# One kernel, a new static order: 1,331 operations rearranged, 54 copies moved between two engines, three warm-up matmuls fewer

## The chip, the core and the metric

The kernel runs on one core of a Trainium2 chip. A core has five instruction streams that run side by side and meet at semaphores: TensorE (PE, matmuls; PEld is its weight load), ScalarE (ACT), VectorE (DVE), GpSimd (POOL), and SyncE (SP), which here issues nearly all DMAs. The metric is device time in microseconds (us) of one execution.

## The reference, cut to what matters

Two attention layers on the same input `x` (2048 tokens by 640, bf16, 32 heads of 20), mixed by a gate:

```
g = sigmoid((x * gate_w).sum(-1))
out = g * A(x) + (1 - g) * B(x)

A: q, k, v from x @ wqkv; phi(t) = [softmax(t @ w_phi), softmax(-t @ w_phi)]
   o = phi(q) @ (phi(k)^T v) / (phi(q) @ sum phi(k)), then o @ wo
B: 4 segments of 512 tokens; in each, causal softmax attention inside the segment,
   plus a memory M, z from the segments before: num / den with phi = elu + 1
   o = sigmoid(beta) * a_mem + (1 - sigmoid(beta)) * a_dot, then o @ wo
```

## The kernel before

The kernel writes its program as a graph. `build_all` creates every operation (a matmul group, one copy, one activation, one DMA) with the tiles that it reads and writes, and `schedule` and `emit` turn the graph into five instruction streams. Nothing is decided by a planner at build time: three constants at the top of the file hold the result of a search made beforehand.

- `ORDER` is one list of all operations, numbered in the order in which `build_all` makes them and written in base 36. Each engine runs its own operations in this order, strictly one after the other.
- `CHOICE` has a digit for each operation that two engines could do: 0 is the first engine named, 1 the second. Copies out of PSUM made by `evac` may be on ACT or DVE. The multiplications `ETr` (line 902 scales oP, line 941 adds the memory part moT, line 1104 scales ET) and `Anorm` (line 973) may be on DVE or POOL.
- `WHERE` has a digit for each tile: the buffer that it takes, or the pair of the eight PSUM banks. An operation that writes a tile waits for all readers of the tile that held its place before.

In `emit`, a wait is put in front of an operation for each producer on another engine that is not yet known to have finished, so whatever stands behind that operation on its engine waits too. This holds for the DMA queue on SP as well.

The work, by the names in the code: B needs `qkproj` (five matmuls of 512 columns, line 647, for segment n, head group c, q or k side), `vproj` (ten matmuls, lines 669 and 670), then for each of 8 head groups per segment the bursts `QK` (lines 774), two `exp` per burst on ACT (line 783), `mask` on POOL (line 787), `PV` on PE (line 815) and a copy `oU_ev`. There are 80 bursts and 160 `exp`. A burst takes four PSUM banks until its two `exp` have read them. A needs `pkA`, `vA`, `Aexp`, `Zred` (line 971), `Zrec` (line 972), `Anorm`, `kv`, and the sum of E in `acc`, called `chain` (line 1013). When all keys are done, for each segment S of queries come `pqA` (line 1067), `qexp` (line 1072), the sums `Zq` (line 1084), and a way through DRAM that spreads the quotient of two sums over the partitions: `Zq_ev`, DMA `zw`, DMA `zr`, `rq` (lines 1095 and 1096, DVE), four DMAs `rw`, one DMA `rr`, `ETr`, and then the matmuls `U` (line 1119) with `Uc` and `Uo` on DVE. `Nmm` (lines 925 and 926), `memc` and `memp` (lines 930 to 933) read the memory of B. `final` (lines 1145 and 1146) is the output projection of one of 16 tiles of 128 tokens; the four of the last segment are split into `finA` and `finB`, joined on DVE (`oadd`, line 1160). `spin` (line 1168) is a matmul of 512 columns whose result nobody reads.

The set-up loads `B_wq` and `B_wk` through `stq` and `stk`, each in a first part (head groups 0 and 1) and a second part (groups 2 to 4), spreads them into `WB` by copies `WBm` and `WBs`, and loads `B_wv` into `WvB`.

Of the kernel before, what the change touches and what calls it, by code (L numbers as in the profile page):

```python
# [36 lines left out]
2w 2x oz oh 78 4s 4t 4u 2p 4x ow 4v oi oj 4z 3j 4j 4y 8a p2 p0 3i 3o 3m 3n 3p 56 79 8b 92 4k qj qk 57 p8 58 77 p1 p9 pb pc 19 51 om on 59 53 52 54 7w
88 5g os 7x 50 ot 5i 76 89 ok 5h 5j 55 7a 5c 5k 7b 5e dq 5d 5f ol 5a dr 67 69 p3 68 7c q8 di q9 dj oo qa pj p4 5l 80 pk 5m 5b 7e pd 5o 5n pe pf 81 5q
5p qd 8c pg 8d 5x pl pv 5y 5z 10r 60 ph pi 5r 5s pw 5t 86 25 5u 87 qe 84 63 64 85 65 pm 7f 6a 6b 7g pn po qg qh pp pq pr ps pt qi ds 8g pu px dt 66 8e
5v py 5w qb 6c qc 6d l pz 6y 61 62 70 6z q0 71 ql q1 6j q2 26 6l 8m do 8n 7d c8 7h 6k 8o 6m qm dp qn 7i 6o 6q 8f 7j dk 1b ca 6p 6f c9 6h 4w q5 dw q6  # L40
qf 1f 6n dl 6r q3 q4 6g 6u dx cb 6i 6w q7 dy 6s 6v 6x qu 8h 1d dz 9c 9e r6 1e 72 6t r7 9d 95 qr 98 qt qv qo 96 qq qs qp 9a 99 cc cd qw 73 e0 74 9r 9t
9s 8p ce qx 8q e1 97 re 8r rf 9h 8i 8s j6 9i 9f 94 qy cg 9j 9k 6e 8t 9g j7 r3 r4 qz rj r5 cf r0 8u hz r1 r2 9n rk rb rl r8 9o 8v 9p rc 8w hw ro rr rd
8l ch ru 8k 9u 9v sh rs rt 8x 9b rv 9l 8j ai 75 9q rp i0 si 9m rq ci hx aj ak 10s r9 ra 7m jc rw ae af ag rx 9w ry rg 9x rh rm jd ri rn 10t a8 j8 sm
s5 s6 a9 aa 9z j9 1c al ah sn so s2 a1 a0 s7 ea 1l s4 eb a2 rz s8 hy i1 s3 ec a3 sr s9 a4 sa sb a5 s0 sc t2 ab t3 se s1 ss t4 t7 am an sf du b5 sg ao
a6 b7 t8 su dv b6 sv sd ed 1i a7 sj sp ac ee sw ef st au sq t5 av sx aw t6 b9 u1 sy bb ba sk sz b8 t0 10u t9 10v sl ad tg 10w dm th t1 ti az dn 10x eg
i2 42 ja b0 b1 eh bc b2 tj tk aq bd ei u0 ar td be te as tf i4 ta jb bh ax tc tb tl tm tn to u8 at i5 bf bi bl ue bj bn ay bm u5 e2 u6 bo ub e3 bp i3
u9 uf ap uc ej ug b3 ek el ud u7 i6 ua u2 2 u3 tp bq tq bs br tr bt jg tt je u4 b4 jh e4 7l bw by bx jf uh e5 1y c0 bz c1 jk ui uj uk ji c2 e6 bk bu
f0 f1 f2 1z 20 e7 jm tx c3 c4 bv c5 jl jj c6 fb fc jn cj fd ff fg fh jy jz k0 1j e8 f5 f7 ul f6 um 9y up 1g ty k1 tz un 43 uo k2 ts jo k4 eq jp 3 i7
1h 29 2a uq 27 fe 8y k3 k5 fi k6 ew ex ey tv 2b tw tu f8 44 e9 ur 1k 2c 28 7k ck cl fj k7 k8 k9 cm fk f3 8z 90 7n 91 d1 c7 i8 us ut i9 d2 7o d3 7p fl
d4 f4 g2 uy v2 ez 7q uz v0 bg 7r g3 g4 uu et cq v1 v3 v4 v6 va vb uv uw vj cn v7 v5 v8 7t f9 fr v9 g5 fa vc vk vl vd cw fs vm ve ft vn vf vo 7s cp cr  # L50
vg cs vh cx cy cz g6 vi g7 g8 co z7 fn em z8 fu fp fo ct db d0 vp dc dd de cv fw d5 fv vq vr g9 fy cu ga d6 fq fx z4 d7 fz ux d8 d9 z5 vs df da dh gb
ge vt vu vv vy vw vx ke gf yy gg gc kh gi g0 dg wr jt gk yz vz gx gj z1 z2 gy gz g1 gt wo wl gu h0 gv gn z3 wi gw ws go h1 gp gq wt w1 gl w0 wm we wf
# [1194 lines left out]
```

## Time and profile before

| | us |
|---|---|
| three runs | 309.72, 310.06, 310.87; median 310.06 |
| the profiled execution, its own time | 308.58 |
| its span, first to last instruction | 306.9 |

The profiled execution thus lies 1.48 below the median, and 1.7 of its time is outside the span. The profile gives each instruction of this one execution a start and a duration. A busy time in a stretch is the part of it in which the engine had work; for PE it counts pipelined matmuls until their modelled end. The granted clock (PEclk) is 1.00 at the higher of TensorE's two levels, 2.4 GHz, and a stretch below 1.00 has been partly at the lower one, 1.2 GHz.

### The profile page before, as it was taken

How to read it: one execution, taken by the hardware profiler on the slowest of the kernel's cores; microseconds unless marked ns; L12 is line 12 of the kernel's file. 1: busy time of each engine (PE TensorE's matmuls, PEld its weight loads, DVE VectorE, ACT ScalarE, POOL GpSimd, SP SyncE). 2: the span in 40 equal slices, each digit the busy share in tenths (PEclk: the TensorE clock that was granted, in tenths of full speed). 3: DMA queues.
4: the chain of work that ended last, by engine and by line, in shares of the span. 5: the costliest groups of instructions: out<-in, count | busy, mean ns of one | idle time of the engine just before them, and what ended most of it. 6: DMA issues, size and time to landing. Idle time of an engine off the chain costs nothing.

```text
span 306.9 us, 7044 instructions
## 1 busy us (share of the span) xinstructions
PE 281.3 (92%) x2882; PEld 149.0 (49%) x2926; DVE 224.6 (73%) x350; ACT 252.9 (82%) x341; POOL 135.7 (44%) x144
## 2 busy tenths in 40 slices
PE   6979999999999999999999899998998779679995
PEld 3435654555555546455445564444543333436752
DVE  2123566898999999999878797735575467876985
ACT  4889999999999999899998979987899997874000
POOL 0322327236680654696323719465342643663030
PEclk9999999999999999999999999999999975979999
DMA  7999960016772740103805635573654556468984
GB/s 183 189 247 259 107 123 16 18 41 96 79 106 68 157 105 0 25 2 107 223 11 144 194 79 134 118 152 109 96 87 127 143 140 184 105 155 244 186 121 171
DMA packets 75816, 37.19 MB, mean 121 GB/s; under 512 B 60136, under 2 KB 72712, under 8 KB 75784
## 3 DMA queue, kind: packets, MB, share of 16 engines
q1 hardware_dynamic: 75688, 36.70, 53.8%
q8 instruction: 23, 0.38, 0.5%
q0 software_dynamic: 96, 0.04, 0.5%
q14 instruction: 9, 0.07, 0.1%
HBM read 13.85 MB, written 12.07 MB: 84 GB/s over the span
## 4 chain that ended last, share of the span: by engine, by line
PE 53%; DVE 21%; ACT 12%; DMA 6%; SPq 4%; issue 3%; POOL 0%; DVEq 0%
PE ps L1145 8%; PE ps L647 7%; PE ps L1067 6%; ACT expT L783 6%; PE ps L958 6%; PE ps L815 5%; PE ps L774 5%; DVE acc L1013 4%; DVE z L971 4%; ACT ej L783 3%; PE ps L1146 3%; PE ps L1119 2%; SPq L486 2%; PE ps L669 2%; DMA stk<-in_B_wk_dram 2%
## 5 line engine op out<-in xcount | busy, mean ns | idle before, releaser
L783 ACT ACTIVATE expT<-ps 128x1024 bf16<-128x1024 f32 x128 | 124.1, 1030 | 11.8 <-PE ps L774 11.2
L787 POOL TENSOR_SCALAR_AFFINE_SELECT expT<-expT 128x512 bf16<-128x512 bf16 x96 | 73.6, 778 | 64.6 <-ACT expT L783 56.9
L647 PE MATMUL ps<-xT,WB 128*128 128x512 bf16 x190 | 45.8, 379 | 3.0 <-ACT WB L626 1.3
L787 POOL TENSOR_SCALAR_AFFINE_SELECT ej<-ej 128x1024 bf16<-128x1024 bf16 x16 | 17.6, 1098 | 41.3 <-ACT ej L783 29.0
L783 ACT ACTIVATE ej<-ps 128x1024 bf16<-128x1024 f32 x32 | 31.2, 1025 | 4.6 <-PE ps L774 4.5
L1013 DVE TENSOR_TENSOR acc<-acc,E 64x1280 bf16<-64x1280 bf16 x31 | 29.6, 955 | 1.0 <-DMA acc<-acc 0.3
L647 PEld LDWEIGHTS ps<-xT,WB 128*128 128x128 bf16 x200 | 17.7, 98 | 23.7 <-issue 2.4
L973 POOL TENSOR_TENSOR E<-E,z 128x1280 bf16<-128x1280 bf16 x9 | 21.1, 2356 | 16.5 <-DVE z L972 16.5
L627 DVE CAST out<-ps 128x640 bf16<-128x640 f32 x12 | 9.9, 822 | 22.7 <-PE ps L1146 22.7
L815 PE MATMUL ps<-expT,v1B 128*32 128x384 bf16 (+2 forms) x384 | 24.4, 322 | 2.2 <-POOL expT L787 1.0
L971 DVE TENSOR_REDUCE z<-E 128x64 f32<-128x1280 bf16 x16 | 23.4, 1469 | 3.4 <-POOL E L973 2.5
L1072 ACT ACTIVATE ET<-ps 128x512 bf16<-128x512 f32 x40 | 22.2, 608 | 2.8 <-PE ps L1067 1.9
L669 PE MATMUL ps<-WvB,xT 128*128 128x512 bf16 x76 | 22.9, 381 | 1.7 <-DMA WvB<-in_B_wv_dram 1.3
L1067 PE MATMUL ps<-xT,WqA 128*128 128x512 bf16 x93 | 22.8, 380 | 1.6 <-DVE out L627 0.6
L774 PE MATMUL ps<-qkm 20*128 20x384 bf16 (+3 forms) x320 | 20.2, 301 | 3.7 <-ACT expT L783 1.7
L1145 PE MATMUL ps<-Wo,oP 128*128 128x512 bf16 x78 | 23.1, 382 | 0.1
L965 ACT ACTIVATE E<-ps 128x640 bf16<-128x640 f32 x32 | 21.9, 725 | 0.4
L958 PE MATMUL ps<-WvA,xT 128*128 128x512 bf16 x76 | 22.1, 380 | 0.0
L1145 PE MATMUL ps<-Wo,oTA 128*128 128x512 bf16 x70 | 21.9, 394 | 0.1
L958 PE MATMUL ps<-WkA,xT 128*128 128x512 bf16 x73 | 21.5, 380 | 0.0
L1146 PE MATMUL ps<-Wo,oTA 128*128 128x128 bf16 x80 | 18.0, 225 | 2.0 <-issue 1.0
L627 DVE CAST oU<-ps 128x512 bf16<-128x512 f32 x23 | 15.7, 684 | 5.3 <-PE ps L815 4.9
(142 smaller groups left out, 566.5 us busy)
## 6 DMA issues: line engine op xcount, KB each, us to landing
opk<-oU SPq DMA_DIRECT2D x16, 256.0 KB
rx<-rc SPq DMA_DIRECT2D x16, 160.0 KB
rr<-rx SPq DMA_DIRECT2D x4, 640.0 KB
out_dram<-out SPq DMA_DIRECT2D x16, 160.0 KB
scr<-qkm SPq DMA_DIRECT2D x16, 120.0 KB
qks<-scr SPq DMA_DIRECT2D x16, 120.0 KB
oP<-opk SPq DMA_DIRECT2D x3, 640.0 KB
WvB<-in_B_wv_dram SPq DMA_DIRECT2D x1, 800.0 KB
```

What stands on the lines that cost most here:

```text
L647: r = e.matmul(self.pf(pt, 0, 0, LSEG), lhsT=self.WB[:, w, kc, 128 * c:128 * (c + 1)], rhs=xT[:, kc, LSEG * n:LSEG * (n + 1)], start=(kc = ...
L669: e.matmul(self.pf(pt, 0, 0, 512), lhsT=l, rhs=self.WvB[:, kc, 0:512], start=(kc == 0), stop=(kc == 4))
L774: r = e.matmul(self.pf(pts[i // 2], i % 2, c0, N), lhsT=view(32 * i, 32 * i + DH, 1, 128 * j, 128 * (j + 1)), rhs=view(32 * i, 32 * i + DH ...
L783: self.op("act", d_act(1024), lambda e, p=p, o=o: e.activation(o(), self.pbanks(pts[p], 0, 2, 512), ACT.Exp, scale=scale), W=[(pts[p], 0), ...
L787: self.op("pool", d_pool(n_el), lambda e: e.affine_select(view(), view(), pattern=pat, compare_op=ALU.is_ge, fill=0.0, base=0, channel_mul ...
L815: r = e.matmul(self.ps[32 * i:32 * i + 32, 512 * ad.t[0] + 128 * j:512 * ad.t[0] + LSEG], lhsT=vt[:, 21 * (H * j + h):21 * (H * j + h) + 3 ...
L958: e.matmul(self.pf(pt, 0, 0, 512), lhsT=l, rhs=W[:, kc, 0:512], start=(kc == 0), stop=(kc == 4))
L971: self.op("dve", 1.48, lambda e: e.tensor_reduce(z[:, :], Ev(), axis=AX.X, op=ALU.add), R=[(E, 0), (E, 1)], W=[(z, "*")], claim=[rz], pr=p ...
L1013: self.op("dve", 0.9, lambda e, src=src: e.tensor_tensor(acc[lo:lo + 64, :], acc[lo:lo + 64, :], src(), ALU.add), R=[(self.Et[t], 0), (sel ...
L1067: r = e.matmul(self.pf(pt, 0, 0, LSEG), lhsT=self.WqA[:, kc, 128 * c:128 * (c + 1)], rhs=xT[:, kc, LSEG * S:LSEG * (S + 1)], start=(kc == ...
L1145: e.matmul(self.pf(pt, 0, 0, 512), lhsT=l, rhs=self.Wo[:, c, 0:512], start=(c == c0), stop=(c == c1 - 1))
L1146: r = e.matmul(self.pf(pt, 1, 0, 128), lhsT=l, rhs=self.Wo[:, c, 512:640], start=(c == c0), stop=(c == c1 - 1))
```

## The change

Only the constants change. `NSPIN` goes from 20 to 17, and `ORDER`, `CHOICE` and `WHERE` are new; the functions, the operations and the tiles are the same. Cut to its first lines:

```diff
-NSPIN = 20
+NSPIN = 17

 ORDER = """
-0 1 10i 10j 10k 10l 5 1a 10m 7 10n s 6 11 w u 4 t x 8 1m v q 9 1n r 10o a 10p 10q 1t 1o 1s 2y b p 32 1u 30 31 c 1p n o 1q 34 2z 46 33 d 1r 36 3a 3b 35
...
+0 1 10i 10j 7 4 10k 10l 6 10m 5 a 1t w x 1s b 8 q u r v s t p 10n 1u 1n 10o 10p o 34 1m 9 30 c 1o 31 d 1r n 32 1q 1p j 2y 33 2z 3e g 4a 3f 36 4c 37 3a
...
-CHOICE = "101000100000000010000110000100001000010011011010011100000011000100111101010011011000000110011011111110010001111111000001111010110100101100010111001011000001010100011000001001001111111111111111"
+CHOICE = "000000000111100101101101010000000100001000101111001011001010011100110111011000000001000100011011111110000011011111000001111110010100000110011110100101110100010100011001001001001111111111001111"
```

Read back into operations (the number behind # is the place in which `build_all` makes operations of that name, from 0; `qkproj` #(10n+2c+w) is segment n, group c, w = 0 for q and 1 for k):

```
engines      DVE to ACT: 25 copies    ACT to DVE: 29 copies
             POOL to DVE: ETr 4, Anorm 2    DVE to POOL: ETr 1, Anorm 3
             of those that ran at 60 to 100 us before: 9 copies to DVE, 2 to ACT, Anorm 1 each way
             of those that ran at 100 to 147 us: 2 copies to DVE, 4 to ACT, Anorm 2 to POOL, 1 to DVE
             oU_ev #28 (ran at 266.0 on ACT): to DVE.  ETr #8 (ran at 267.5 on POOL): to DVE
             the copies of final 10 and 11, and oU_ev #31: to ACT

SP start     before: .. x1, stk second part (2 DMAs), WvB, wkT ..
             after:  .. x1, WvB, stk second part (2 DMAs), wkT ..

PE start     before: 6 spin, xtr 1 3 2 0, 3 spin, qkproj 0 2 1 3, QK, 4 6 12, QK, 10 8,
                     vproj 0, QK, qkproj 5 7, fuse 1 2, vproj 1, fuse 3 4, qkproj 9, QK, fuse 0, qkproj 14, vproj 2, QK, pkA 1
             after:  5 spin, xtr 3 0 2 1, 3 spin, qkproj 3 1 2 0 8, QK, 4 6, QK, 10 14,
                     vproj 0, qkproj 12, vproj 1, QK, qkproj 5 7 9, fuse 3 1 0 4, spin, QK, fuse 2, vproj 2, QK, vproj 3, pkA 1

PE, from final 4 to final 8
             before: final 4, QK, PV, QK, pqA 18, PV, QK, spin, Nmm 5, spin, QK, Nmm 4, QK, Nmm 6, spin, QK, PV, QK, og, PV, QK, spin,
                     Zq 3, QK, U 11, QK, U 10, QK, U 8, PV, Nmm 7, U 9, QK, PV, QK, QK, final 8
             after:  final 4, QK, pqA 18, PV, QK, spin, PV, QK, Nmm 5, QK, spin, spin, Nmm 4, QK, Nmm 6, spin, QK, og, spin, PV, QK, PV, QK,
                     Zq 3, QK, U 9, QK, U 8, QK, U 10, U 11, PV, QK, PV, QK, Nmm 7, QK, final 8

DVE, from Zq_ev 2 to ETr 18
             before: Zq_ev 2, oU 22, g, out_ev 4, oU 25, rq 4 5, omg, iomg, oU 24, memc memp 5, 4, 6, oU 26, rqr, rqm, pqmin 4, oU 27, ETr 18
             after:  Zq_ev 2, oU 22, pqt1 5, pqmin 5, eg, iomg, pqmin 2, rq 4 5, out_ev 4, oU 24, oU 25, memc memp 5, 4, pqmin 4, memp 6,
                     rqr, rqm, oU 26, ETr 18
SP there     before: rw rw rw rw rr;  after: rw rw dr out rw opw 12 rw rr   (opw 12 stores what oU 24 and oU 25 copied)

DVE, end     before: .. rrB, out_ev 9, memc 9, Uc 14, memp 9, Uo 14, ETr 13, fa, fa, fa, ETr 10, ETr 12, oadd ..
             after:  .. rrB, out_ev 9, Uc 13, memc 9, Uo 13, fa, ETr 13, memp 9, fa, ETr 10, fa, ETr 12, oadd, oadd, fa, oadd, oadd
```

Of the 17 remaining `spin`, eight stand ahead of the first `qkproj`, one among the `fuse` groups, three between 60 and 160 us and five between `final` 4 and `Zq` 3 (before: nine, none, seven and four).

## Rows read from the trace of the kernel before

**Rows 1.** The page's first part: busy time, share of the span, instructions.

```profile
PE 281.3 (92%) x2882; PEld 149.0 (49%) x2926; DVE 224.6 (73%) x350; ACT 252.9 (82%) x341; POOL 135.7 (44%) x144
```

**Rows 2.** Windows: stretch, length, busy us (instructions) by engine, clock, DMA share, GB/s.

```profile
30.00:60.00 30.00, 29.52 (x287) 15.37 (x291) 21.02 (x26) 29.61 (x43) 13.38 (x15) 1.00 0.45 70
60.00:100.00 40.00, 38.91 (x419) 21.75 (x425) 36.49 (x45) 38.99 (x53) 19.03 (x18) 1.00 0.50 79
100.00:147.00 47.00, 45.63 (x442) 24.84 (x449) 46.11 (x57) 44.47 (x62) 29.81 (x25) 1.00 0.27 67
147.00:180.00 33.00, 30.85 (x356) 15.91 (x360) 26.85 (x61) 30.32 (x45) 13.18 (x16) 1.00 0.47 130
180.00:230.00 50.00, 48.33 (x492) 25.15 (x501) 32.63 (x50) 43.13 (x58) 25.22 (x23) 1.00 0.56 117
...
280.00:292.00 12.00, 11.80 (x179) 8.62 (x178) 11.92 (x25) 0.60 (x1) 0.85 (x2) 1.00 0.88 212
```

**Rows 3.** Windows of the late stretch, same columns.

```profile
230.00:246.00 16.00, 12.55 (x155) 5.90 (x161) 7.24 (x13) 14.85 (x18) 7.11 (x11) 1.00 0.48 142
246.00:261.00 15.00, 12.97 (x152) 5.18 (x144) 10.52 (x18) 12.67 (x15) 5.97 (x8) 0.66 0.60 156
261.00:276.00 15.00, 10.88 (x138) 6.02 (x136) 11.91 (x21) 11.91 (x14) 10.44 (x11) 0.89 0.55 128
```

**Rows 4.** Timeline of the start: start, us, instruction, [idle before, what ended it].

```profile
12.69 3.19 PE L647 MATMUL ps<-xT,WB 128*128 128x512 bf16 x14 [0.49 <-ACT WB L626]
...
17.45 0.80 ACT L626 ACTIVATE WB<-stk 128x720 bf16<-128x720 bf16 x1 [0.16 <-DMA stk<-in_B_wk_dram]
...
19.76 0.39 PE L669 MATMUL ps<-WvB,xT 128*128 128x512 bf16 x1 [1.29 <-DMA WvB<-in_B_wv_dram]
...
21.25 0.40 PE L774 MATMUL ps<-qkm 20*128 20x384 bf16 x8
...
22.32 1.89 PE L647 MATMUL ps<-xT,WB 128*128 128x512 bf16 x8 [0.67 <-ACT gh L577]
```

**Rows 5.** Groups of one shape on DVE: busy, mean ns, idle before, releaser.

```profile
L627 DVE CAST qkm<-ps 128x512 bf16<-128x512 f32 x15 | 10.1, 683 | 9.5 <-PE ps L647 9.4
...
L627 DVE CAST vA<-ps 128x640 bf16<-128x640 f32 x5 | 4.1, 820 | 1.9 <-PE ps L959 1.9
...
L755 DVE TENSOR_TENSOR pq<-pq,tmp 128x1536 bf16<-128x1536 bf16 x3 | 2.9, 953 | 0.0
...
L753 DVE TENSOR_SCALAR tmp<-qkm 128x1024 bf16<-128x1024 bf16 x3 | 2.7, 904 | 0.0
...
L941 DVE TENSOR_TENSOR oP<-oP,moT 128x1280 bf16<-128x1280 bf16 x3 | 2.5, 847 | 2.6 <-DMA moT<-mo 2.0 <-DVE oP L902 0.6
...
L755 DVE TENSOR_TENSOR pq<-pq,tmp 128x1024 bf16<-128x1024 bf16 x3 | 2.1, 684 | 0.0
```

**Rows 6.** Timeline around the last bursts, final 8 and its input.

```profile
266.03 0.60 ACT L626 ACTIVATE oU<-ps 128x512 bf16<-128x512 f32 x1
...
267.51 2.61 POOL L941 TENSOR_TENSOR oP<-oP,moT 128x1280 bf16<-128x1280 bf16 x1
...
271.13 0.63 PE L1145 MATMUL ps<-Wo,oTA 128*128 128x512 bf16 x1
...
275.43 1.94 ACT L783 ACTIVATE ej<-ps 128x1024 bf16<-128x1024 f32 x2 [2.14 <-PE ps L774]
```

**Rows 7.** Timeline of DVE between Zq 2 and U.

```profile
241.85 0.82 DVE L627 CAST out<-ps 128x640 bf16<-128x640 f32 x1 [4.29 <-PE ps L1146]
...
257.44 1.55 DVE L1104 TENSOR_TENSOR ET<-ET,rr 128x1536 bf16<-128x1536 bf16 x2
```

**Rows 8.** Timeline of SP's DMA queue, the same stretch.

```profile
250.73 0.36 SPq L486 DMA_DIRECT2D rr<-rx  x1
```

**Rows 9.** The chain that ended last, in order of time: start, us, what.

```profile
171.51 5.05 DMA rr<-rx
...
296.76 2.13 DMA moT<-mo
```

More of the change, by code (lines that the diff above doesn't have):

```diff
@@ L37 @@
[L37 to L52, printed above, removed]
@@ new lines @@
+35 3b 46 48 e 17 7u 7v 47 4b 82 83 49 3q 3r f h 7y 3t m 7z 3s 1w 1v 4f 4g i 1x 38 3u 11 4h 3c y z 10 13 16 15 12 4d 14 2d 3g 3d 39 3v 3h 2k 2l 2g 2e
+2f 2h 2m 2n 10q 76 4p 4r 4q 2i 4s 3k 2j 3w 3x 4t 18 4l 7a 3z 3y 3l 3j 21 4m 4n 4o op 40 2q 41 oq 77 2r 2w 4e ox 2s or 3i 3p 3m 3o 3n 92 22 p5 2x 2t oy
+78 p6 oz 2o 2p 24 p0 23 p7 p1 pa pb 4i ou 2u 2v 4j 4x pc 4u 4k 4z oh 4y 8a 4v 56 93 ov oi oj 8b 7w 58 7x p8 om on 1a 57 k 5g p9 ok 5h oo qj 5i 51 ol
+4w qk dq 52 ow 59 53 pj 84 pk 5c 79 50 q8 7b 5d q9 5e qa 5j 85 5k 8c p2 os ot 19 7c p3 p4 pl 8d 86 87 54 55 5a 5b 67 5f 69 68 5l 88 pm 5m pd 89 7e pf
@@ new lines @@
+pe pn po pp 5x pq 6a 5z 5y 80 pg 81 5o 5q 5p 60 di dr pv dj pi ph 5s 5t 5u 10r 7f 7g 5v qg pw 6b pr 63 64 ds r6 65 66 qh 5r qi ps qd 7d cc c8 dt 5w 6c
+r7 qe ql pt 6d 8f pu 6y 25 6z 70 61 62 71 q0 qm q1 px q2 py 72 6j q3 q4 6k 8m 6l 8e pz 8n 6o qn 6m 6p 7h 8g 8o 6q q5 6f dw 6g qb 6r 8h 6h 7j 6i 7i 6u
+qc cb 95 6n q6 dy qf q7 c9 dx do 6w 6s 6v dp 6x 8i ca 9c 9e qu dk 9d 6t 73 dl qo 74 qv dz qp qq 98 qr qs 99 9a qt cd 8p 9h 8q qw e0 8r 9j qx 9f qy 9i
+ce re cg 9g 9r e1 rf 9k 9s cf qz 9t 8k 96 9u r3 rj 8s rk r0 r1 r4 8t 8u rb r5 8v 94 r2 8l l rl rc 5n rd 9n 26 8w 9b rr 9o ch 9p rs 8x 9v 9q ru rt sh
@@ new lines @@
+u0 ub uc bk u2 u3 jg el ud bq u4 br 10t bs bo jh uh bw by bx tt 1f jk 1g bp bt ui tp tq ts c0 8y c2 ji bu tr jl fb c1 c3 1i bg 8z i3 1y bz bv c4 fc fd
+jm e2 jj ff fg e4 c5 c6 fh jn cj f0 f2 f1 fe jy jz k0 f5 f7 f6 fi k1 k2 k3 ew ex tw uj ap k4 uk ul k5 e9 1j f8 um k6 uq e6 tz i7 un ey up uo k7 e8 e7
+tv 1k 7n ur c7 et 42 90 1h fj jo k8 43 k9 jp tx ty 1z 20 28 29 27 2c 2a tu 2b 7k ck fk cl cm g2 i8 44 ut i9 7o us 7p uu 91 f3 fl g3 v6 v2 g4 uv eq uw
+uy vj v3 vk v7 g5 v4 vl vd jt d1 v8 7q cq uz ez co v0 ve d2 d3 vf cn f4 v5 va vb f9 vc d4 7r fr fs cp ft cr vm fa 7t cw cx cy cz vn 7s vg vh vo v9 g6
@@ new lines @@
+g7 z7 g8 fn vi vp fp fo z8 d5 ux cs fw fx g9 d6 vq fy ga v1 ct cu fz d7 db dc dd vr d0 z4 fu ke d8 vs gb d9 de gi z5 vt da vu df fv vy gk vv fq gc yy
+cv yz vw gj ge gf dg dh wr gg g0 gx gz g1 gy z1 gn eu h0 h1 vx vz ws wt wu jr z2 w0 w1 gp gt gu gv gd wo go wi gw wj gh we wv w6 wf wg wl w2 w7 wp w8
+wk w9 gq h2 wq wa ww wm w3 xq w4 xw wb wn xr xs xx wc ho wh h3 zd hq xy js ze hp gl hk hl hm y2 gm hr gr he zj hs em kh hf gs hg h9 hn xt y3 hb ha wd
+en ia eo hh zk jq jv y4 ht hu er ev xu h5 zg zh w5 h6 h7 h8 kz kf xv l1 jw l3 l0 l5 jx wx hc hd hi l4 kt kv wy ju z9 hj ku kk za km ko ki kj kl ka kq
@@ new lines @@
+kp l6 xz l7 ep l2 y0 y1 kw l8 lf lh lg 10u kn kr ks es wz hv x0 h4 x1 kx x2 zb li lk ll ip ky l9 lm lb lc ld fm 10v 10w ln ik x5 iq ir x3 is lj lu lv
+ib zf iu x4 lw la x6 il le x7 lx 10x im in lq lr ie ls ly iv 10y lt it io lo zl kg iw ix id mh lz if lp ig x8 mi mb x9 y5 y6 ic mj mc m6 md m7 m8 m0
+iy xe me m2 m3 m4 xf xg y7 xa xb z3 xc m9 ml mn mm xi mk xh xj xk xm m5 ma mo xn mp mf n9 na nb mq xd xo n3 n5 n4 iz n6 nc ih mg mr ii j0 my j4 zm m1
+xl n0 mz mu mw mv y8 j1 j2 z6 nq mx y9 ya ms ij zn nd mt j3 j5 zs kb ne kc kd nv nw n1 n2 n7 nx ny yd yb nf 45 ng nh ni yc ye zt xp nj o5 oa n8 o6 o7
@@ L69 @@
+023207512436730023020583014503031130512203010003210000670011237103415030440100053210126013201816034525000160020000701105323160023321281036121730023410
+03250423120362003003652221408373201033202100641210100303114227330314283
 """
```

24 lines of the change are left out of this document (9 added, 15 removed).

## The prediction, made before the changed kernel was run

> **What bounds the kernel now.** I read the page's first part, then the same totals by stretch of time, then the start, the late stretch and the chain that ended last. Over the whole span PE is busy for 281.3 of 306.9 us and ACT for 252.9 [rows 1]. That PE is at 92% doesn't say that it is always the limit, so the stretches come next [rows 2]. From 30 to 147 us three engines are full together: at 60 to 100 us PE has 38.91 of 40, ACT 38.99 and DVE 36.49; at 100 to 147 us PE has 45.63 of 47, DVE 46.11 and ACT 44.47. From 180 to 230 us PE is full (48.33 of 50) and ACT has nearly 7 us to spare. From 230 to 276 us it is the other way round [rows 3]: ACT has 14.85 of 16 at first while PE has 12.55, and PE falls to the lower of its two clock levels, granted 0.66 at 246 to 261 us and 0.89 at 261 to 276 us. From 280 us on PE is full again (11.80 of 12), and so is DVE (11.92) [rows 2].
>
> Work that no order removes is therefore nearly all of the time. What an order can win is PE's idle time where PE is the limit, and ACT's idle time from 230 to 280 us. From 30 to 230 us PE is idle for 0.48 + 1.09 + 1.37 + 2.15 + 1.67 = 6.8 us in 200 [rows 2], so this long part holds little. Before 30 us and after 230 us there is more.
>
> The sums below are made against the profiled execution, 308.58 us; the median of three runs is 310.06, so 1.48 is added at the end. Differences under 0.5%, 1.55 us, can hardly be told from no change.
>
> **The change, part by part.**
>
> Start. PE waits 0.49 us for a copy of WB, 1.29 us for WvB to land, and 0.67 us before qkproj 5 [rows 4], 2.45 in all. The first engine to be late is the DMA: WvB lands at about 19.7, the second part of stk at 17.4, where its last copy starts. The new order sends WvB first and the second part of stk behind it, so their places should about swap: WvB near 17.5, stk near 19.7. The matmul side is turned to suit: qkproj 8 fills the first gap, qkproj 14 stands ahead of vproj 0, and qkproj 12 and vproj 1 stand between vproj 0 and qkproj 5, which needs stk. A qkproj costs 3.19 × 5/14 = 1.1 us and a vproj at most 21.25 − 19.76 = 1.5 us [rows 4], so 1.1 + 1.1 + 1.5 us of work and a burst lie in front of qkproj 5 from the time that WvB lands. That covers stk's delay of 2.2 us and its copies. I take −2.3 us of the 2.45. Below nothing, 0 if the transfers only change which of them is late; above, −3.0, since ten copies leave ACT and eight come to it before 30 us.
>
> 30 to 230 us. Here PE's own sequence changes in small swaps and keeps its length; the copies that change engine cost PE nothing as long as DVE and ACT cover them. From 60 to 100 us DVE gets nine copies and gives two: seven times the mean of 0.683 and 0.820 us [rows 5] is +5.3 us, and it has 40 − 36.49 = 3.5 us free [rows 2]. From 100 to 147 us it gives more than it gets (four copies against two, one Anorm less), and it had gaps before 60 us (21.02 of 30). So the load is moved forward on DVE by 1.8 us more than fits, and fits later. I take 0, with −2.5 (a third of the 6.8 us) and +1.8 as bounds.
>
> 230 to 280 us, set by ACT. The order of the bursts against `final` 6, 4 and 8 is the same: as many bursts stand between them as before, so ACT doesn't get ahead. What it gains is one oU copy of 0.60 us that goes to DVE, and some of the 2.14 us that ACT waited at 275.43 behind final 8 [rows 6]. final 8 was then partly at the lower clock: its matmuls of 512 columns took 0.63 us. Its last input, a sum on POOL of 2.61 us that ended at 270.1, goes to DVE at 0.85 [rows 5, 6], but stands there behind two oU copies (0.68 each) and another ETr, so final 8 is hardly earlier. I take −0.6 − 0.4 = −1.0. Bounds: −5.4, which is all of ACT's idle time from 246 to 276 us (2.33 + 3.09) [rows 3], and +2.2 if the way to U gets longer (below).
>
> **The clock** in this stretch is the largest single item. The rows show granted 0.66 and 0.89 over 15 us each, which makes 2 × 15 × (0.34 + 0.11) = 13.5 us at 1.2 GHz, after a stretch in which PE was idle for 3.45 of 16 us [rows 3]. With five spin in place of four and the same groups between them, I expect nearly the same share of low clock. The Trainium skill, in TensorE: Matmul & The Clock Gate, section Terms, prices such time at its length times the share of pulses left out, so half of it: 6.8 us, and its way to the same fall (section HAM oscillation) is idle PE between bursts. By that rule, spins that held the clock would be worth 6.8 us, where ACT's idle time bounds it at 5.4; the trace speaks for the smaller one, since ACT, not PE, sets the pace there.
>
> The end. PE is full until the last finB, with the same groups. Two copies of final outputs and one oU leave DVE for the idle ACT, and memp 9 moves behind ETr 13. The transpose that follows memp 9 left SP's queue only at 296.76 and took 2.13 us [rows 9], so most of that shift is hidden by SP; without this cover it would cost the 0.85 of ETr 13 [rows 5]. I take +0.3, bounds −0.5 and +1.5.
>
> Sum: −2.3 + 0 − 1.0 + 0.3 = −3.0, so 305.6 profiled and 307.1 as a median. With terms missing each other by about 1.5, this case alone spans 305.3 to 308.4.
>
> **The rivals.**
>
> DVE hides it. If DVE's 1.8 us too many at 60 to 100 us reach PE through PSUM banks freed late, the sum is −1.2: 308.9. For it: three engines full at once. Against it: PE had its small gaps there already, and DVE has slack before and after. Also the case that the new order is simply no shorter ends here.
>
> The way to U gets longer. Between Zq_ev 2 and rq 4 the new order puts pqt1 5, pqmin 5 and pqmin 2 on DVE (0.90 + 0.68 + 0.95) [rows 5], and on SP it puts opw 12 in front of the last rw and rr: it waits for two oU copies (1.4). Behind them stand out_ev 4, whose PSUM a burst needs, and U 9, which stands in front of bursts on PE. 3.9 us of new work, less the 1.7 us that were free (rr left at 250.73, 5.05 us of flight as in the earlier one, ETr 18 at 257.44 [rows 7 to 9]), is +2.2: 309.3. Against it: DVE was idle for 4.29 us just there, waiting for final 4 [rows 7], and the DMAs zw and zr have to be waited for anyway.
>
> The low clock comes later, where PE is the limit: the rival that ends slower. In 246 to 261 us it cost little since ACT set the pace. One such period is 2 × 0.34 × 15 = 10.2 us long [rows 3]; falling into the full stretch from 276 us on, it would cost half, 5.1 us: 312.2. For it: PE is idle for 4.1 of 15 us just before [rows 3], final 8 now waits on a longer DVE queue, and the five spin stand earlier, with none behind PV 5. It decides if PEclk is under 1.00 at any slice behind 280 us.
>
> The clock holds. If the five spin keep PE at 2.4 GHz from 246 us on, more of the 5.4 us comes back; I take 3 of them: 304.1.
>
> **How the numbers follow.** Main case 0.45, clock holds 0.13: these two are faster by over 1.55 us (under 308.5), 0.58. DVE hides it 0.14 and longer way to U 0.10: within 0.5%, 0.24. Low clock at the end 0.18: slower. The likeliest is the main case, 307.1. For 8 in 10 the range must reach into both outer cases: 303.0 leaves out about half of the one where the clock holds, 312.0 a little over half of the slow one, together under 0.2.
>
> **What would show it.** Start: qkproj 5 with vproj 1 and qkproj 14 done before it, near 22 us; wrong if PE waits over 1.5 us for stk or WvB. Middle: bursts of segment 2 about 2 us earlier than before; wrong if DVE's copies stand before PE's waits at 60 to 147 us. Late: ACT's idle time from 246 to 280 us near 5 us and the low clock again at some 10 us; wrong if it is gone or lies behind 276 us. End: some 24 us from the last exp to the last finB. The prediction fails as a whole if the 2 us of the start don't reach 230 us, or if a new wait for rr opens in front of U 9.

## The result, and the profile after

The changed kernel takes 313.12 us (median of 20 runs, 310.64 to 315.83) beside 309.89 us for the kernel before (20 runs): ratio 1.0107 [1.0082, 1.0132], slower by 3.2 us. Medians here and below are of all runs of a kernel, ratios of its fast runs alone, so the two don't always divide out. The forecast was 307.1 with 303.0 to 312.0 as its range. The profiled execution took 313.95 us, 5.37 more than the one of before; the two traces thus differ by 2.1 us more than the medians do.

The page's first part and its row of the granted clock, kernel after [rows 1]:

```profile
PE 287.1 (92%) x2923; PEld 149.6 (48%) x2923; DVE 226.5 (73%) x356; ACT 251.3 (80%) x337; POOL 128.8 (41%) x142
...
PEclk9999999999999999999999999999999977977999
```

The windows of the kernel after, columns as in [rows 2, 3]:

```profile
30.00:60.00 30.00, 30.00 (x292) 15.70 (x289) 23.07 (x28) 29.26 (x42) 17.31 (x18) 1.00 0.42 75
60.00:100.00 40.00, 39.61 (x422) 21.12 (x420) 36.55 (x50) 37.49 (x47) 17.14 (x19) 1.00 0.35 48
100.00:147.00 47.00, 43.74 (x419) 22.80 (x418) 43.55 (x51) 42.20 (x62) 30.79 (x23) 1.00 0.36 75
147.00:180.00 33.00, 30.77 (x345) 15.31 (x345) 25.43 (x60) 29.82 (x44) 12.67 (x17) 1.00 0.55 155
180.00:230.00 50.00, 47.14 (x511) 24.70 (x504) 31.48 (x55) 40.06 (x53) 18.60 (x21) 1.00 0.57 105
230.00:246.00 16.00, 13.79 (x140) 6.48 (x139) 10.81 (x15) 15.25 (x19) 8.10 (x10) 1.00 0.34 92
246.00:261.00 15.00, 12.44 (x158) 5.08 (x156) 10.69 (x19) 13.13 (x16) 7.19 (x11) 0.77 0.67 170
261.00:276.00 15.00, 11.07 (x167) 5.92 (x156) 12.04 (x20) 14.08 (x16) 6.50 (x9) 0.95 0.82 181
276.00:292.00 16.00, 15.03 (x174) 9.04 (x173) 8.62 (x21) 6.27 (x9) 3.09 (x5) 0.83 0.84 169
```

The row to stop at is 100 to 147 us. PE has 43.74 where it had 45.63, DVE 43.55 where it had 46.11, ACT 42.20 where it had 44.47 [rows 2]: all three are busy for some 2 us less in the same 47, so each waits more. At 60 to 100 us, where the forecast put 5.3 us of copies on top of DVE's load, DVE has 36.55, hardly more than its 36.49 before: the copies came, but the sums of E there fell from eleven, 11.2 us in all, to ten, 9.1 us.

Windows of the same times don't hold the same work, so I laid the two traces side by side by work: wherever both orders have done the same set of matmul groups on PE (fillers not counted), a cut is made, and the stretch between two cuts is compared. The last row ends with the issue of the last output DMA on SP. In us; the first column is the time in the kernel before:

```
cut to cut    before   after   after - before   h5 (before's order from 42 us)   f3 (before's order 42 to 170 us)
0   to 44      44.30    42.81    -1.49             42.65                             42.35
44  to 94      49.53    49.71    +0.18             50.13                             50.13
94  to 124     29.86    30.14    +0.28             29.86                             29.87
124 to 171     47.76    50.91    +3.15             47.74                             49.04
171 to 190     18.22    18.06    -0.16             18.22                             17.80
190 to 218     27.93    29.85    +1.92             27.91                             28.04
218 to 239     21.31    21.85    +0.54             21.31                             21.85
239 to 276     37.14    35.74    -1.40             37.22                             36.05
276 to 293     17.10    20.22    +3.12             16.98                             18.42
293 to end     11.56    10.95    -0.61             12.11                             10.95
sum           304.72   310.25    +5.53            304.13                            304.48
```

The start, kernel after, timeline of PE [rows 4]:

```profile
7.73 5.57 PE L647 MATMUL ps<-xT,WB 128*128 128x512 bf16 x25 [1.52 <-DVE WB L627]
...
18.32 0.38 PE L669 MATMUL ps<-WvB,xT 128*128 128x512 bf16 x1
...
22.26 0.40 PE L774 MATMUL ps<-qkm 20*128 20x256 bf16 x8
```

vproj 0 starts at 18.32 instead of 19.76 and doesn't wait for WvB; nothing waits ahead of the bursts at 22 us. One wait of 1.52 us for a copy of WB is left, at the very start.

The dearest stretch, kernel after, timeline of DVE, POOL and PE:

```profile
117.43 3.36 DVE L1013 TENSOR_TENSOR acc<-acc,E 64x1280 bf16<-64x1280 bf16 x4
...
125.03 2.25 DVE L1013 TENSOR_TENSOR acc<-acc,E 64x1280 bf16<-64x1280 bf16 x2 [1.47 <-DMA acc<-acc]
...
129.22 2.39 DVE L1013 TENSOR_TENSOR acc<-acc,E 64x1280 bf16<-64x1280 bf16 x1
131.65 0.61 DVE L1001 TENSOR_TENSOR KVZacc<-KVZacc,ps 128x440 f32<-128x440 f32 x1
...
127.95 2.99 POOL L973 TENSOR_TENSOR E<-E,z 128x1280 bf16<-128x1280 bf16 x1 [0.17 <-DVE z L972]
...
132.32 0.39 PE L774 MATMUL ps<-qks 20*128 20x512 bf16 x4 [2.44 <-DVE KVZacc L1001]
```

DVE waits 1.47 us for a DMA from acc to acc (`accmove` 2). Then one sum takes 2.39 us, nearly three times the 0.84 of the four at 117.43: it starts 1.27 us into POOL's multiplication and ends at 131.61, 0.67 us after that has ended (130.94). The sum into KVZacc stands behind it, and PE, which needs its PSUM bank, waits 2.44 us.

The chain that ended last, kernel after [rows 9]:

```profile
120.81 4.19 DMA acc<-acc
...
129.22 2.39 DVE acc L1013
...
197.41 3.99 DMA zb<-zs
201.42 2.57 DMA zc<-zb
...
207.31 2.71 DMA rx<-rc
210.03 4.71 DMA rr<-rx
```

The chain runs through both these DVE steps and, in segment 2, through the way over DRAM, where `zw` (zb<-zs) takes 3.99 us; in the kernel before it took 2.3.

The last outputs, kernel after, timeline of PE [rows 6]:

```profile
274.27 0.38 PE L1145 MATMUL ps<-Wo,oTA 128*128 128x512 bf16 x1 [0.47 <-DVE oP L941]
...
282.15 0.63 PE L1145 MATMUL ps<-Wo,oTA 128*128 128x512 bf16 x1
...
285.36 0.38 PE L1145 MATMUL ps<-Wo,oP 128*128 128x512 bf16 x1
```

The low clock ends later: a matmul of `final` 10 at 282.15 still takes 0.63 us, as one of `final` 8 did before.

### The profile page after: what moved, and what is told of

Its sections match the earlier page's. It is cut to its first block, busy times and chain, and to the rows that moved or that the text cites. A ratio compares the mean times of both kernels' runs of the same rounds, so it can differ in the third digit from the quotient of the medians.

```text
span 312.2 us, 7072 instructions
## 1 busy us (share of the span) xinstructions
PE 287.1 (92%) x2923; PEld 149.6 (48%) x2923; DVE 226.5 (73%) x356; ACT 251.3 (80%) x337; POOL 128.8 (41%) x142
## 4 chain that ended last, share of the span: by engine, by line
PE 55%; DVE 16%; ACT 15%; DMA 8%; issue 3%; SPq 1%; POOL 0%
PE ps L647 10%; ACT expT L783 9%; PE ps L1145 9%; PE ps L958 9%; DVE acc L1013 5%; PE ps L1067 4%; PE ps L774 4%; PE ps L815 4%; PE ps L669 4%; ACT ej L783 3%; PE ps L1146 2%; PE ps L959 2%; ACT ET L1072 2%; PE ps L1119 2%; DVE E L973 2%
## 5 line engine op out<-in xcount | busy, mean ns | idle before, releaser
L787 POOL TENSOR_SCALAR_AFFINE_SELECT expT<-expT 128x512 bf16<-128x512 bf16 x96 | 70.3, 742 | 100.5 <-ACT expT L783 91.2
L647 PE MATMUL ps<-xT,WB 128*128 128x512 bf16 x200 | 48.1, 380 | 2.0 <-DVE WB L627 1.5
L787 POOL TENSOR_SCALAR_AFFINE_SELECT ej<-ej 128x1024 bf16<-128x1024 bf16 x16 | 19.1, 1191 | 32.3 <-ACT ej L783 28.4
L973 POOL TENSOR_TENSOR E<-E,z 128x1280 bf16<-128x1280 bf16 x10 | 24.1, 2416 | 11.4 <-DVE z L972 11.4
L1145 PE MATMUL ps<-Wo,oTA 128*128 128x512 bf16 x80 | 25.5, 406 | 2.4 <-DMA oTA<-oA 0.5
L815 PE MATMUL ps<-expT,v1B 128*32 128x512 bf16 (+2 forms) x384 | 24.6, 321 | 0.6 <-POOL expT L787 0.6
L1067 PE MATMUL ps<-xT,WqA 128*128 128x512 bf16 x100 | 24.3, 380 | 0.0
L774 PE MATMUL ps<-qkm 20*128 20x128 bf16 (+3 forms) x320 | 20.2, 301 | 4.1 <-ACT expT L783 1.5
L958 PE MATMUL ps<-WkA,xT 128*128 128x512 bf16 x80 | 23.2, 380 | 0.1
L627 DVE CAST qkm<-ps 128x512 bf16<-128x512 f32 x14 | 9.6, 688 | 13.5 <-PE ps L647 13.4
```

Source lines behind the costliest of these rows:

```text
L647: r = e.matmul(self.pf(pt, 0, 0, LSEG), lhsT=self.WB[:, w, kc, 128 * c:128 * (c + 1)], rhs=xT[:, kc, LSEG * n:LSEG * (n + 1)], start=(kc = ...
L774: r = e.matmul(self.pf(pts[i // 2], i % 2, c0, N), lhsT=view(32 * i, 32 * i + DH, 1, 128 * j, 128 * (j + 1)), rhs=view(32 * i, 32 * i + DH ...
L787: self.op("pool", d_pool(n_el), lambda e: e.affine_select(view(), view(), pattern=pat, compare_op=ALU.is_ge, fill=0.0, base=0, channel_mul ...
L815: r = e.matmul(self.ps[32 * i:32 * i + 32, 512 * ad.t[0] + 128 * j:512 * ad.t[0] + LSEG], lhsT=vt[:, 21 * (H * j + h):21 * (H * j + h) + 3 ...
L958: e.matmul(self.pf(pt, 0, 0, 512), lhsT=l, rhs=W[:, kc, 0:512], start=(kc == 0), stop=(kc == 4))
L973: self.op(("dve", "pool"), {"pool": d_pool(1280, 2), "dve": 1.56}, lambda e: e.tensor_tensor(Ev(), Ev(), rz[:, :].rearrange("p (h o) -> p ...
```

## The experiments

But for the number of fillers (`spin`), and for one operation that is done twice in t1, t2 and t3, all kernels hold the same operations. A is the changed kernel's ORDER, B the one of before; an operation's CHOICE and WHERE digits come from the order that it is taken from. Of most, a rival expectation stood beside the main one. Medians and ratios to the kernel before, run on the same chip:

```
h1_start_after      320.76  1.0374 [1.0320, 1.0427]    h6_after_to_158     316.19  1.0156 [1.0107, 1.0205]
h2_start_before     317.75  1.0272 [1.0216, 1.0328]    h7_after_from_158   313.64  1.0105 [1.0061, 1.0150]
h3_after_to_192     316.09  1.0225 [1.0164, 1.0285]    h8_middle_before    311.14  1.0028 [0.9992, 1.0064]
h4_after_from_192   318.35  1.0286 [1.0221, 1.0351]    m3_transpose_ahead  311.73  1.0049 [1.0015, 1.0084]
h5_start42_after    308.46  0.9946 [0.9920, 0.9972]    f1_start_and_tail   308.51  0.9971 [0.9944, 0.9998]
m1_kvacc_early      313.37  1.0107 [1.0071, 1.0142]    t1_dve_twice        312.12  1.0074 [1.0044, 1.0105]
m2_opw_early        313.17  1.0085 [1.0048, 1.0121]    t2_act_twice        309.91  0.9983 [0.9948, 1.0018]
s1_spins_after      313.36  1.0106 [1.0072, 1.0140]    t3_pe_twice         312.68  1.0094 [1.0061, 1.0128]
f2_anorm_on_pool    312.29  1.0071 [1.0039, 1.0103]    f3_seam_at_176      308.74  0.9967 [0.9944, 0.9991]
```

**Halves of the two orders.** Where does the loss lie? One order up to a cut, the other behind it:

```diff
-ORDER = A
+ORDER = A[:300] + [o for o in B if o not in A[:300]]    # h1; h2 the same with B first, 303
+ORDER = A[:860] + [o for o in B if o not in A[:860]]    # h3; h4 the same with B first, 863
```

> The changed kernel's order, engines and buffers for the first 300 operations (about the first 70 us), the order of the kernel before from there. Theory A (the start gains 1.5 us by the traces at 70 us, the losses come later and have their own places): 308.4 us, ratio to before about 0.995. Rival B (what the start gains is given back at the first later wait, whatever follows): 309.9, ratio 1.000. Rival C (the whole difference is where the low clock falls in the last 50 us): 309.9 too, but with other granted clocks in the rows after 230 us than the kernel before.

> The mirror of the last one: the order of the kernel before for the first 70 us, the changed order from there. Theory A: the changed kernel's 313.1 us plus the 1.5 us of the start, 314.6, ratio to before 1.015. Rival B: 313.1, ratio 1.010.

> The changed order for the first 860 operations (about 192 us), the order of the kernel before from there. Theory A (by the traces the changed kernel is 2.0 us behind at 192 us, from the DVE and DMA waits at 124 to 132 us): 311.9 us, ratio 1.006. Rival C (all of the loss is in the last part): 308.4 to 309.9, ratio 1.000 or less.

> The order of the kernel before for the first 192 us, the changed order from there. Theory A (3.3 us of the changed kernel's 5.3 us in the profiled pair come after 192 us, 1.9 at 196 to 217 us and 2.3 at 274 to 286 us, of which the second hangs on where the low clock falls): 311.3 to 313.2 us, ratio 1.005 to 1.011. Rival C: 313.1, ratio 1.010. Against both: 309.9, ratio 1.000, which would put the loss ahead of 192 us.

All four came out slower than either kernel, so none of the theories' numbers was met and nothing is decided. A seam, the place where one order passes into the other, isn't free: there tiles of one order meet buffers and PSUM banks chosen for the other. h1 lost some 10 us between 64 and 96 us, right behind its seam, and stood 9.6 us behind the kernel before from there to 220 us.

**The start alone, and three suspects.** A cut in a quiet place, at 42 us, and three single edits of the changed kernel:

```diff
+ORDER = A[:190] + [o for o in B if o not in A[:190]]    # h5
-DVE: .. chain 20 .. chain 23, kvacc 8, .. kvacc 9       # m1
+DVE: .. kvacc 9, kvacc 8, chain 20 .. chain 23
-SP:  .. accmove 2, .. opw 3, opw 2                      # m2
+SP:  .. opw 3, opw 2, accmove 2
-NSPIN = 17                                              # s1: 22 more fillers late in the program
+NSPIN = 39
```

> As the first of the joined orders, but with the changed order for the first 190 operations alone (about 42 us), and where a buffer of the one order is taken in the other, the free one that has been idle longest. The first joined kernel lost 10 us at its seam, from 64 to 96 us, and carried them unchanged to the end. Theory A (the start gains 1.5 us in its own right and is carried like the loss was): 308.4 us, ratio 0.995, if the seam costs nothing. Rival B: 309.9. If the seam costs again, the difference to the kernel before at 35 us, ahead of the seam, and at 100 us, behind it, tells the two apart.

> The changed kernel with only kvacc 9 and kvacc 8 moved on DVE, from behind chain 22 and chain 23 to ahead of chain 20, into the 1.47 us that DVE idles there. Theory A (in the changed kernel the burst QK1,7 waits 2.44 us for the PSUM banks that kvacc 8 frees at 132.26 us, and a shift at 96 us of a run before was carried unchanged to the end): 310.7 us, 2.4 less than the changed kernel's 313.1, ratio to before 1.003. Rival D (the wait goes over to what stands next, chain 23 and the E buffers that ACT's Aexp writes): 312.5 to 313.1, ratio 1.009.

> The changed kernel with only the two oP writes 3 and 2 (256 KB together) moved on SP, from right behind accmove 2 to ahead of it, into idle time of SP and of the transfers at 116 to 120 us. Theory A (accmove 2 takes 3.7 us from issue to its reader in the changed kernel and 2.2 at most in the kernel before because it shares the transfers): chain 20 starts 1.4 us earlier, 311.7 us, ratio to before 1.006. Rival D (PE's burst QK1,7 hangs on kvacc 8 behind chain 22, 23 and the POOL work beside them, not on chain 20): under 0.5 us of gain, 312.6 to 313.1.

> The changed kernel with 22 more of its filler products of 512 columns on TensorE, set into gaps of 0.3 to 1.0 us that TensorE has between 239 and 282 us; nothing else is changed. Theory C (in the last part the two kernels differ by where the low clock falls: final 8 and final 10 take 4.25 us each at 1.2 GHz and 2.56 at 2.4 GHz): if the fillers keep the clock up, 3.4 us less on final 8 and final 10 alone, 309.7 us, granted clock over 0.99 and ratio to before 0.999. Rival: the clock falls all the same, and the fillers cost some of their 22 x 0.22 us, 313.1 to 315.

h5 has the lowest ratio of the study, 0.9946 [0.992, 0.9972]: against the kernel before it has the new start alone, and in its trace it keeps 1.06 to 1.1 us of it from 90 to 260 us, as the main expectation had it, and 0.59 at the end. Windows of h5; the engines are full again where the changed kernel was not:

```profile
100.00:147.00 47.00, 46.35 (x453) 24.74 (x455) 46.09 (x58) 44.47 (x63) 29.74 (x25) 1.00 0.28 66
...
180.00:230.00 50.00, 48.98 (x499) 24.53 (x497) 32.98 (x48) 43.12 (x58) 25.78 (x24) 1.00 0.58 120
```

m1 moved forward what PE waited for, and it gave nothing, as its rival had it: the 2.48 us won between the groups that stand around it (20.46 to 17.98) came back as 2.17 behind them (30.45 to 32.62). Timeline of DVE in m1, sums of two operands beside POOL:

```profile
126.38 4.05 DVE L1013 TENSOR_TENSOR acc<-acc,E 64x1280 bf16<-64x1280 bf16 x2
...
137.09 3.12 DVE L1013 TENSOR_TENSOR acc<-acc,E 64x1280 bf16<-64x1280 bf16 x2
```

Two sums that take 1.65 us undisturbed took 4.05 and 3.12 here. m2 shortened the way of accmove 2 to 3.32 us and shows nothing: the 0.7 us that its trace has less there turned up in m3 too, which lacks the edit. In s1 the mean granted clock was 0.987 to 0.995, in the changed kernel's executions 0.971 to 0.994, and s1 was no faster, as its rival had it. The four executions of the changed kernel at 0.989 or more took 310.64 to 311.25 us, the four of s1 that were so high 312.24 to 314.06: at the same clock the fillers cost some 2 us, about as much as the clock gave.

**Halves again, at other cuts, and the transpose.**

```diff
+ORDER = A[:670] + rest of B                             # h6
+ORDER = B[:695] + rest of A                             # h7
+ORDER = A[:190] + B up to 235 us + rest of A            # h8
-SP: .. zw 1, oTB 0, zr 1                                # m3
+SP: .. oTB 0, zw 1, zr 1
```

> The changed order, engines and buffers for the first 670 operations (to about 158 us), the order of the kernel before from there. Theory A (delays are carried unchanged; by the traces the changed kernel is 1.3 us behind there, 1.5 ahead from its start and 2.8 behind from the stretch at 124 to 132 us): 311.2 us, ratio 1.004. Rival E (the loss comes back after 132 us, as it did when kvacc 8 was moved): 308.4 to 309.9, ratio 0.995 to 1.000.

> The mirror: the order of the kernel before to about 159 us, the changed order from there. Theory A: what the changed kernel loses behind 158 us, 1.9 us by the medians (3.2 less 1.3) and up to 4.0 by the profiled pair: 311.8 to 313.9 us, ratio 1.006 to 1.013. Rival E: 313 and more, since all of the loss would be here, ratio 1.010 or over.

> The changed order to 42 us, the order of the kernel before from there to 235 us, the changed order in the last 75 us. Theory A (with 308.5 us for the changed start on the order of before, and by the profiled pair 0.9 us more loss behind 235 us): 309.4 us, ratio 0.998. Rival C (the low clock falls on final 10 in the changed tail, 1.7 us, and its two waits ahead of it, 0.9): 311.0 us, ratio 1.004. Against both (the tail is no loss): 308.5, ratio 0.995.

> The changed kernel with only the transposing transfer oTB 0 moved on SP, from right behind the write zw 1 of the denominators to ahead of it, so that it doesn't run beside it. Theory A (zw 1 to zr 1 takes 4.0 us in the changed kernel and 2.3 in the kernel before, and the products U 7 to U 4 hang on it): 1.5 us less, 311.6 us, ratio 1.005. Rival F (the kernel before has a transposing transfer at the same place, so it isn't that; what is late is the evacuation ahead of it): within 0.4 us of the changed kernel, 312.7 to 313.5.

h6 is slower than the kernel before, though not clear of the changed one (the intervals overlap); a seam explains it as well as a theory would. h7 and h8 hold one filler more whose product lies in another PSUM bank. The waits of PE in h7 at 111 to 122 us show its cost:

```profile
PE ps L1168 <- ACT expT L783: 1.3, 1, 1.3
PE ps L1168 <- ACT vA L626: 0.8, 1, 0.8
```

L1168 is the filler. It does nothing useful, but waits until ACT has read the bank, and PE lost 2.3 us there. So h7 and h8 carry a cost that belongs to neither order. m3 moved the transpose that stood on SP between `zw` and `zr`; zw's way stayed at 3.95 us, so the transpose wasn't its cause. Its median is 1.4 us under the changed kernel's, for which I have no cause.

**Start and tail, and what a microsecond costs in the middle.** f1 is h8 with its fillers in banks that PE needn't wait for, and the cut at 238 us. t1, t2 and t3 are the kernel before with one operation done twice:

```diff
+ORDER = A[:190] + B up to 238 us + rest of A            # f1
+Zred 8 (DVE, 1.47 us) once more into a spare tile       # t1
+Aexp 16, half of it (ACT, 0.70 us) twice                # t2
+vA 12 (PE, 1.24 us) twice                               # t3
```

> The changed order for the first 42 us, the order of the kernel before from there to 238 us, the changed order in the last 70 us; unlike in the run with the middle of before, each filler product keeps the PSUM bank that it has in its own kernel (a filler in another bank waited for ACT there and cost 2.3 us at 112 us). Theory A, with all parts additive: start 1.9 us less, the tail of the changed order 0 to 1.5 us less by the traces so far: 306.5 to 308.0 us, ratio 0.989 to 0.994. Rival C (the changed tail costs 1 to 2 us because the low clock falls on final 10): 309.0 to 310.0, ratio 0.997 to 1.000.

> The kernel before with one more operation on DVE: the sum Zred 8 (1.47 us at 105 us) is done a second time, its first result goes to a spare tile. Theory G (DVE sets the pace from 93 to 154 us, since it idles 0.3 us there): all later work moves by 1.4 to 1.5 us to the end, 311.4 us, ratio 1.005. Rival H (TensorE or ACT sets it): under 0.4 us, 309.9 to 310.3.

> The kernel before with one more operation on ACT: the exponential Aexp 16 (0.70 us at 102.6 us) is done a second time, the first time into the half that Aexp 17 overwrites. Theory G: ACT has 2.2 us of gaps up to 154 us, so behind 154 us nothing is later by more than 0.3 us: 309.9 to 310.2. Rival H (ACT sets the pace): all later work moves by 0.6 to 0.7 us, 310.6, ratio 1.002.

> The kernel before with one more group of products on TensorE: vA 12 (1.24 us at 109.6 us) is done a second time into the same banks. Theory G: TensorE has 5.9 us of gaps up to 154 us, so behind 154 us nothing is later by more than 0.3 us: 309.9 to 310.2. Rival H (TensorE sets the pace): all later work moves by 1.2 us, 311.1, ratio 1.004.

f1 and h5 agree (308.51 and 308.46), so the changed tail, from 238 us on, neither wins nor loses by what could be timed. Timeline of DVE in t1, the added reduce (L169) and its original:

```profile
104.77 1.47 DVE L169 TENSOR_REDUCE two<-E 128x64 f32<-128x1280 bf16 x1
106.16 1.47 DVE L974 TENSOR_REDUCE z<-E 128x64 f32<-128x1280 bf16 x1
```

Against the kernel before, PE's groups start 0.16 us earlier ahead of it and 1.45 us later behind it: 1.61 us for an operation of 1.47, carried on to 240 us. t3: 1.39 us for 1.24 (from -0.06 to +1.33, read at 154 us on DVE's starts; its profiled execution, 317.08 us, was the longest of its four and is read up to 179 us only). What came out at the end is more: by the ratios 2.3 us [1.4, 3.3] for t1 and 2.9 [1.9, 4.0] for t3. In t1's trace a further 1.7 us are lost at 241 us, where `final` 4 falls into the low clock (granted 0.89 at 230 to 246 us; 1.00 in the kernel before). t2: in the profile 0.99 us for 0.70, but the timed ratio, 0.9983, shows nothing, so for ACT this stays unresolved. In this stretch, then, DVE and PE have no slack, though [rows 2] has PE idle for 1.37 us of it.

**One multiplication back to POOL, and the middle alone.**

```diff
-CHOICE digit of Anorm 11: 0 (DVE)                       # f2
+CHOICE digit of Anorm 11: 1 (POOL)
+ORDER = A[:190] + B up to 170 us + rest of A            # f3
```

> The changed kernel with one multiply, Anorm 11, back on POOL, where the kernel before has it; on DVE it took 2.07 us at 114.8 us. Theory I (every engine's work in that stretch is carried to the end, since the in-order queues wait on each other): 2.07 us less on DVE, of which POOL's 2.35 us beside the chain of sums takes back 0.5 to 1: 311.5 to 312.1 us, ratio 1.006. Rival J (chain 19, which needs Anorm 11, now waits for POOL, which is busy to 117.4 us): 313 to 314.

> The changed order for the first 42 us, the order of the kernel before to the 176th group of products (about 170 us), the changed order from there. Theory K (the changed order loses 1.75 us between the groups 198 and 245, by the times of that stretch in eight runs of the one order and six of the other, and the rest of its loss between 98 and 176): 308.5 us of the run with start and tail plus 1.75, 310.2 us, ratio 1.002. Rival L (the loss at 198 to 245 is only what the late arrival there makes of it): 308.5, ratio 0.997.

f2 took 2.07 us off DVE in a stretch with no slack, and the stretch (94 to 124 us) kept its length, as the rival had it: 30.15 and 30.14 us. Timeline of DVE and POOL in f2:

```profile
115.81 0.69 DVE L627 CAST qkm<-ps 128x512 bf16<-128x512 f32 x1 [1.38 <-PE ps L647]
116.42 4.63 DVE L1013 TENSOR_TENSOR acc<-acc,E 64x1280 bf16<-64x1280 bf16 x4
...
108.20 9.29 POOL L973 TENSOR_TENSOR E<-E,z 128x1280 bf16<-128x1280 bf16 x4
```

DVE now waits 1.38 us for PE, and its next four sums take 4.63 us where they took 3.36 at 117.43 in the changed kernel: the first of them starts while POOL's last multiplication runs, which ends at 117.49. The f2 median is lower than that of the changed kernel by 0.8 us; its interval and that one's overlap.

But for some buffers at the seams and four fillers, f3 differs from the changed kernel only between 42 and 170 us, and it is 4.4 us faster than it (308.74 against 313.12); from h5 it differs only behind 170 us, and they can't be told apart (0.9967 and 0.9946, intervals overlap). So the loss is made between 42 and 170 us. (What f3 itself has over before at 124 to 171 us, 1.28, all lies behind 168.8 us, at its seam.) The chain that ended last in f3:

```profile
194.95 2.59 DMA zb<-zs
197.56 2.24 DMA zc<-zb
```

With the same order behind 170 us, `zw` takes 2.59 us instead of 3.99, and 190 to 218 us takes 28.04 us, 0.11 over before. The 1.92 us that the changed kernel lost there thus don't belong to the order of that stretch.

## Why the prediction was wrong, step by step

**Start, -2.3: right, a little smaller.** -1.49 us in the profiled execution, -1.65 in h5, -1.95 in f3, and -1.5 in the timed runs of h5 (308.46 against 309.98). WvB and the second part of stk changed places as worked out. The condition that these microseconds reach 230 us holds in h5 and fails in the changed kernel, by what comes next.

**30 to 230 us, 0 with a bound of +1.8: the step that failed.** The forecast said that "the load is moved forward on DVE by 1.8 us more than fits, and fits later". From 44 to 239 us the changed kernel lost +5.91 us: 0.18 + 0.28 + 3.15 - 0.16 + 1.92 + 0.54. Three readings were at fault.

The first is that DVE's idle time is room. At 60 to 100 us, where the forecast looked, the copies cost 0.18 us. The loss came behind it, at 124 to 171 us, where three engines stand in a circle: PE waits for a bank that DVE frees, DVE for a product of PE or a DMA, ACT for bursts. There a busy share of 98% on DVE and 97% on PE [rows 2] leaves nothing, and t1 and t3 show it on the kernel before: 1.47 us more on DVE came out as 1.61 behind the stretch, 1.24 more on PE as 1.39, and at the end as more still. A bound from the sum of free time, 1.8 us, was of the wrong kind, since an order can also make engines wait that had been full.

The second is that durations are the same wherever an operation stands. The sum at 129.22 takes 2.39 us instead of 0.82, and the reason goes with its place: POOL is multiplying. Groups of DVE, the kernel before at 93.8 to 153.7 us, then the kernel after at 93 to 157 us:

```profile
L1013 DVE TENSOR_TENSOR acc<-acc,E 64x1280 bf16<-64x1280 bf16 x22 | 20.0, 910 | 0.8 <-DMA acc<-acc 0.3
...
L1013 DVE TENSOR_TENSOR acc<-acc,E 64x1280 bf16<-64x1280 bf16 x22 | 21.9, 994 | 2.0 <-DMA acc<-acc 1.5
```

The same 22 sums take 19.6 to 20.0 us in the eleven kernels with before's order at 93 to 150 us (before, h1, h4, h5, h7, h8, f1, f3, t1, t2, t3), and 21.6 to 23.2 us in the nine with the changed one (after, h2, h3, h6, m1, m2, m3, s1, f2).

The third is that "PE's own sequence changes in small swaps". Between 42 and 170 us the two orders have done the same set of matmul groups at only 21 of 130 places, with up to 25 groups in a row rearranged; behind 170 us it is 53 of 127.

What stays open: which of the waits at 124 to 171 us carries how much of the 3.15 us, and whether PE's new sequence or DVE's load makes them, since f3 puts both back at once. Three single repairs (m1, m2, f2) each removed what they were aimed at and the time went to the next wait; only the whole order of the kernel before, 42 to 170 us, gave it back (f3). A run that removes the overlap of POOL and the sums, with all else kept, wasn't made.

**230 to 280 us, -1.0: right in size.** -1.40 from 239 to 276 us. The gain is work that left ACT and not idle time: in the stretch of the same work (239.1 to 276.05 us before, 243.3 to 279.1 after) ACT is busy for 30.95 and 29.92 us and idle for 6.00 and 5.88. So the 0.6 for a copy was right in kind, and the 0.4 behind `final` 8 isn't seen. But it didn't reach the end: f1, with this part of the new order, is no faster than h5 without it.

**The end, +0.3: too small in the profiled execution.** 276 us to the end took 2.51 more. Of it 1.69 is `final` 10, which ran for 4.25 us and not 2.56, since its matmuls fell into the low clock from 281.4 to 284.8. About the 0.8 left is the order's: f3, with the same order and a clock of 1.00 from 276 to 292 us, has 0.71 over before in the last two rows.

**The rivals.** "The low clock comes later" put the time at 312.2, nearest to what came, and its mark is there: PEclk is under 1.00 behind 280 us. It isn't the cause of the loss all the same. At the same mean clock the changed kernel is still slower: at 0.978 three of its executions took 312.89 to 314.48 us and 42 of the kernel before 308.36 to 311.86; at 0.989 and more four took 310.64 to 311.25 and six of before 306.51 to 309.22. The low pieces add up to 13.65 us in both profiled executions; f1 also has 0.89 at 276 to 292 us and equals h5, which has 1.00 there; and f3 wins 4.4 us over the changed kernel by an edit that ends at 170 us. "The clock holds" priced that at 3 us, which was about right, though it didn't come: the changed kernel's executions at 0.989 and more have a median of 311.1 us, its ten at 0.978 and less 313.8. "The way to U gets longer" was wrong in place and in cause: it lengthened in segment 2, and in the DMA `zw` itself (2.3 to 3.99 us), not in segment 3, where rr to `ETr` took 4.98 us and not 6.71. "DVE hides it" named the right engine at the wrong time, and 308.9 was too low.

By the runs the sum is: start -1.5 (h5), 42 to 170 us with what it sets off in segment 2 +4.4 (after less f3), 170 us to the end +0.3 (f3 less h5, within the noise). That it makes the +3.2 that was measured (313.12 less 309.89) shows nothing, since each kernel but the first and the last stands in it once with either sign.

One sum of the forecast doesn't come out: 307.1 with 1.5 either way is 305.6 to 308.6, not 305.3 to 308.4. Its range didn't hang on it.

## What to carry to other kernels

Where three engines are full together, an idle microsecond on one of them is no room: put one operation in twice there and see what comes out at the end, before a move is costed at nothing. When a large reordering moves the time little, replace stretches of it at quiet cuts (few live buffers, the same filler banks) and compare starts of the same groups; here the first 42 us were worth keeping and the rest not, and that kernel (h5, 0.9946 of before) beats both. Price a two-operand sum by the POOL instruction that runs when it starts, not by its mean.
